# Attention and feed-forward on one core: attention pairs two at a time

## The chip, the cores and the metric

The kernel runs on one core of a Trainium2 chip. A core has five engines with queues of their own: TensorE (PE, matrix products into PSUM), VectorE (DVE), ScalarE (ACT), GpSimd (POOL) and SyncE (SP, which here only issues DMA transfers). Each works its own instructions off in the order in which the program gives them; semaphores make one wait for another. The metric is the device time of one execution in microseconds.

## The reference

Eight sequences of 448 tokens, with 12 heads of 64, all in 32-bit floats:

```
rmsnorm(x, g) = x / sqrt(mean(x*x) + 1e-6) * g
attn = softmax(rmsnorm(q, g_q) @ rmsnorm(k, g_k).T / sqrt(64)) @ v     # per sequence and head
x    = attn, the 12 heads side by side: 3584 tokens x 768
xn   = rmsnorm over the 768, times rms_g
g    = xn @ w_gate;  val = xn @ w_val                                # 768 x 1536 each
out  = (g * sigmoid(g) * val) @ w_out                                # 1536 x 768
```

## The kernel before

**Pairs.** Two heads of one sequence make a pair; g counts the 48 pairs, six to a sequence. Two heads fill the 128 rows of TensorE, so scores and values run as 64x64 products on quarters of its array, four at a time, while the feed-forward part uses the whole array.

**A step of the attention.** The 448 keys of a pair are cut in 7 parts. `step(g, i)` (L826) makes the scores of pair g for part i (L805), the weighted values of the pair before, g - 1, for the same part (L823), and, on ScalarE, the exponentials of the new scores (L813, or L811 from sequence 5 on, where q and k come in another layout, the "turned" one). So the values of pair g are added up while pair g + 1 is scored. One pair is seven such steps, 14 rows on TensorE, since a product of 32-bit floats takes two passes. Scores take PSUM banks from a pool of four (`ps_s`), the values the single bank of `ps_m`, which the transposes of q and k use too, and the feed-forward part three banks (`ps_f`). Exponentials take 11 buffers.

**Sums.** The denominators of the softmax are sums over all keys. GpSimd adds the seven exponentials of a pair into one tile (`later_sums`, L904 and L909: six additions), TensorE adds up the 128 rows (`totals`, L887, or in a folded form L867 after VectorE has folded the tile), and VectorE inverts them (L739 to L741). That is done at every even g for the two pairs before it. An odd pair's values are copied out of PSUM unscaled (`hold`, L772); an even step's are multiplied at once (`weigh`, L780), which also has ScalarE square the result and GpSimd add the squares up for the later norm (L783 to L786).

**Feed-forward.** While sequence b is in the attention, sequence b - 1 or the one before is in the feed-forward part, as a list of "products" (`todo`), each one to two microseconds of TensorE. `fill()` takes a sixteenth of a block's list, `fill(n)` takes n. From the second sequence on, gate and value products come from a scheme with 15 products in place of 18 for each of four groups (`three`, products L1419, evacuations L1434 to L1440, the last steps L1451 and L1452, called hand), and the output products from similar schemes with 7 in place of 8, once (`out_strassen`, L1693) or twice nested (`out_quads`, L1778). Both need sums of left operands, which VectorE makes ahead of them (L1492, L989 for x; L1610, L1638 for the output). Such sums are given to the queue one after a product, from the lists `first_sums` and `slow`. In the first sequences VectorE, ScalarE and GpSimd also convert the weights from 64-bit floats (`convert`, one step after each product).

**Time in steps.** `pe(fn)` counts one step, runs fn and then whatever `after(n, ...)` had put n steps ahead. `light(fn)` gives small work of VectorE to a list from which one is taken after each product; `hurry_light` empties it.

**The main loop** (L2143 to L2200) goes over g. For a pair inside a sequence: the attention of pair g, a `fill()`, the preparation of q and k of the next pairs, `fill()`, `fill()`. The last product before an even pair holds its conversion back until the first step of the attention. For the first pair of a sequence (hp = 0) comes the seam: the last ten products of the list (`LEFT = 10`) lie behind its attention, as 3, 2, 1 and the rest; between them stand the fold and the sum of the squares of x (`fold_x`, L922, and `rms_x`, L928 or L937), then `begin` puts the next block's list in place, `norm_x` (L949 or L953) spreads 1/rms, VectorE scales x (L959, six scalings), and a `fill()` follows.

**Places in SBUF.** One tile, `yard`, holds q, k, v and small rows at offsets written out by hand (`AT_...`). In the turned layout, the inverse norms of a pair (`rs`) stand in one of two places.

Of the kernel before, what the change touches and what calls it, by code (L numbers as in the profile page):

```python
# [8 lines left out]
F32 = mybir.dt.float32  # L9
# [326 lines left out]
def safe_scores(  # L336
# [85 lines left out]
    AT_QK = PER_B  # L422
    AT_V = AT_QK + 3 * PAIR
    AT_OTHER = AT_V + 3 * THIRD
    AT_RS = AT_V
    AT_V1 = AT_RS + 7 * NB
# [38 lines left out]
    def squares_turned(g):  # L465

        qk, n = st["qk", g], 2 * NB
        ms = st["ms", g] = spot(AT_RS, 2 * n).rearrange("p (a n) -> p a n", a=2)
        rs = st["rs", g] = spot(AT_RS + (4 + g % 2) * NB + g % 2 * NB // 2, NB + NB // 2)
# [345 lines left out]
    def weighted(g, i):  # L815

        b, hp = divmod(g, NPAIR)
        if i == 0:
            st["av", g] = ps_m.tile([128, 512], F32, name="av", tag="m")
        for j in range(2):  # L820
            r = across(j)
            vt = st["v", g][r, i] if turned(g) else st["vr", b][r, hp] if i == PARTS - 1 else st["v", g][r, i // NK, i % NK]
            nc.tensor.matmul(st["av", g][own(j), 0:S], lhsT=vt, rhs=st["e", g, i][r], start=i == 0, stop=i == PARTS - 1,  # L823
                             skip_group_check=True)

    def step(g, i):  # L826
# [2 lines left out]
        weighted(g - 1, i)  # L829
        if ps is not None:  # L830
            exps(g, i, ps)

    AT_ALIKE = AT_OTHER
    AT_FEW = AT_ALIKE + 128

    def late(g):

# [24 lines left out]
    def totals_folded(g):  # L862

        which = (g - 1, g)
        den = ps_s.tile([128, 512], F32, name="den", tag="s")[:, 0:2 * NB]
        for j in range(2):
            nc.tensor.matmul(den[own(j)], lhsT=alike()[across(j), own(j)], rhs=some_few(0, 2)[across(j)], start=True, stop=True)  # L867
        few = some_few(2, 2)
        nc.vector.reciprocal(few, den)
        for i in which:  # L870
            rd = st["rd", i] = tmp.tile([128, S], F32, name="rd", tag="rd", bufs=2)
            nc.vector.transpose(out=blocks(rd), in_=few[:, i % 2 * NB:(i % 2 + 1) * NB].unsqueeze(2).to_broadcast([128, NB, 32]))
            if i < g:
                weigh(i, 3, 4)

    def totals(g):

# [17 lines left out]
        for i in which[::-1]:  # L895
            invert(st["rd", i], st["rd", i])
            if i < g:
                weigh(i, 3, 4)

    def later_sums(g, n):  # L900

        def first():
            st["es", g] = tmp.tile([128, S], F32, name="es", tag="es", bufs=2)
            nc.gpsimd.tensor_tensor(st["es", g], st["e", g, 0], st["e", g, 1], ALU.add)  # L904
            more(2)

        def more(*parts):
            for i in parts:
                nc.gpsimd.tensor_tensor(st["es", g], st["es", g], st["e", g, i], ALU.add)  # L909

        after(n, first)
        after(n + 2, lambda: more(3, 4))
        after(n + 3, lambda: more(5, 6))
        if folded(g):
            after(n + 8, lambda: light(lambda: fold(g)))

# [1143 lines left out]
            convert()  # L2060


    at_once(squares(0, 0))
    warm(15)
    reduce, root, scale = norm_rests(0, 0, 2)
# [16 lines left out]
    for g in range(NG + 1):  # L2082
# [51 lines left out]
        if g == NPAIR + 1:  # L2134
# [8 lines left out]
            later_sums(g, 2)  # L2143
            begin(0, 15)
        else:
            hurry_light()
            sums_due = g % 2 == 0
            pe(lambda: (totals(g - 1) if sums_due else None, step(g, 0)))
            if st.pop("held", None):
                convert()  # L2150
            pe(lambda: [step(g, i) for i in (1, 2)])
            derive_q()
            pe(lambda: [step(g, i) for i in (3, 4)])
            pe(lambda: ([step(g, i) for i in (5, 6)], weigh(g - 1, 2) if sums_due else hold(g - 1)))
            if g < NG:
                later_sums(g, 11 if g == 3 * NPAIR else 2)
        st["block"] = now["t"]
        for n in (1, 2):
            if turned(g + n) == (n == 1):
                after(2, lambda g=g + n: load_v(g))  # L2160
        if hp:
            fill()
            norm_k(g + 1, 0)
            if not turned(g + 2):
                squares(g + 2, 0)
                squares(g + 2, 1)
            turn_for(g + 1, 0)
            if turned(g + 2):
                squares(g + 2, 0)
            norm_k(g + 1, 1)  # L2170
            some_rests(g)
            fill()
            turn_for(g + 1, 1)
            fill(hold=g % 2 == 1)
            continue
        fill(3)
        norm_k(g + 1, 0)
        if g == TURNED * NPAIR:
            one_per_quarter()
        fill(2)  # L2180
        if late(g):
            fold_x(b - 1)
        turn_for(g + 1, 0)
        norm_k(g + 1, 1)
        fill(1)
        if not late(g):
            pe(lambda: rms_x(b - 1))
        squares(g + 2, 0)
        squares(g + 2, 1)
        turn_for(g + 1, 1)  # L2190
        if late(g):
            fill(min(2, len(todo)))
            pe(lambda: rms_x(b - 1))
        fill(len(todo))
        begin(b - 1, 16)
        pe(lambda: norm_x(b - 1))
        fill()
    fill(len(todo))
    for _ in range(5):
        pe(idle)  # L2200
# [38 lines left out]
```

## Time and profile before

| | |
|---|---|
| Median of 3 runs | 1476.36 us (1475.61 to 1476.56) |
| Profiled execution | 1474.93 us, of which the span from the first to the last instruction is 1473.1 |
| Busy, TensorE | 1453.9 us (99%) |
| Busy, VectorE | 1073.0 us (73%) |
| Busy, GpSimd | 763.9 us (52%) |
| Busy, ScalarE | 620.1 us (42%) |
| DMA | 322.52 MB, 219 GB/s in the mean |
| Granted clock of TensorE | 0.999 |

The profile is one execution. A row of a timeline merges like instructions that follow each other on an engine: start in microseconds from the span's start, length, engine, line of the kernel, operation, output<-inputs by the program's names, shapes, and xcount. Where the engine was idle before it, a bracket gives for how long and what ended it. A row of the groups has the count, then the busy time in microseconds and the mean of one in nanoseconds, then the engine's idle time just before those instructions and what ended most of it. Matmuls are pipelined and their ends are modelled, so a row's length is more than its share of the stream: differences of starts are what counts on TensorE.

### The profile page before, as it was taken

How to read it: one execution, taken by the hardware profiler on the slowest of the kernel's cores; microseconds unless marked ns; L12 is line 12 of the kernel's file. 1: busy time of each engine (PE TensorE's matmuls, PEld its weight loads, DVE VectorE, ACT ScalarE, POOL GpSimd, SP SyncE). 2: the span in 40 equal slices, each digit the busy share in tenths (PEclk: the TensorE clock that was granted, in tenths of full speed). 3: DMA queues.
4: the chain of work that ended last, by engine and by line, in shares of the span. 5: the costliest groups of instructions: out<-in, count | busy, mean ns of one | idle time of the engine just before them, and what ended most of it. 6: DMA issues, size and time to landing. Idle time of an engine off the chain costs nothing.

```text
span 1473.1 us, 25744 instructions
## 1 busy us (share of the span) xinstructions
PE 1453.9 (99%) x8538; PEld 1142.2 (78%) x8538; DVE 1073.0 (73%) x1868; ACT 620.1 (42%) x1551; POOL 763.9 (52%) x684
## 2 busy tenths in 40 slices
PE   9999999999999999999999999999999999999998
PEld 4344445678855788887888889859898799899998
DVE  6788999799975677874579855755679755784665
ACT  7856776455423444234442443444542533101110
POOL 6867997647343363462545744655645842120003
PEclk9999999999999999999999999999999999999999
DMA  8758676776787999777656866677467855597576
GB/s 218 225 158 250 185 240 184 216 252 226 260 267 225 307 314 319 241 248 207 154 165 199 263 191 184 184 227 203 131 191 222 274 171 149 162 305 237 169 231 203
DMA packets 340577, 322.52 MB, mean 219 GB/s; under 512 B 126932, under 2 KB 282068, under 8 KB 340436
## 3 DMA queue, kind: packets, MB, share of 16 engines
q1 hardware_dynamic: 339428, 320.48, 72.9%
q8 instruction: 71, 1.16, 0.3%
q14 instruction: 70, 0.57, 0.1%
q10 hardware_dynamic: 880, 0.30, 0.1%
q0 software_dynamic: 128, 0.00, 0.0%
HBM read 266.90 MB, written 53.77 MB: 218 GB/s over the span
## 4 chain that ended last, share of the span: by engine, by line


## 5 line engine op out<-in xcount | busy, mean ns | idle before, releaser
L909 POOL TENSOR_TENSOR es<-es,e 128x448 f32<-128x448 f32 x205 | 254.5, 1241 | 13.6
L1419 PE MATMUL ff<-x,w 128*128 128x224 f32 x1296 | 258.1, 353 | 0.3 <-DVE pc L1440 0.3
L1419 PEld LDWEIGHTS ff<-x,w 128*128 128x128 f32 x1296 | 243.6, 190 | 3.5 <-issue 2.1
L805 PE MATMUL sc<-qT,kT 64*64 64x448 f32 x1176 | 231.5, 539 | 0.6 <-DVE x L959 0.5
L823 PE MATMUL av<-e,yard 64*64 64x448 f32 x1148 | 224.3, 538 | 0.0
L1419 PE MATMUL ff<-xs,w 128*128 128x224 f32 x832 | 164.5, 353 | 2.7 <-DMA w<-kept 1.9
L1419 PEld LDWEIGHTS ff<-xs,w 128*128 128x128 f32 x832 | 156.3, 190 | 6.2 <-issue 2.1
L805 PEld LDWEIGHTS sc<-qT,kT 64*64 64x64 f32 x1176 | 78.8, 133 | 87.2 <-issue 53.8
L786 POOL TENSOR_TENSOR ss<-ss,rd 128x448 f32<-128x448 f32 x40 | 47.7, 1192 | 157.8 <-ACT rd L785 156.4
L1778 PE MATMUL ff<-w,l 128*128 128x192 f32 x630 | 116.7, 328 | 2.8 <-DVE l L1638 2.2
L1440 DVE TENSOR_TENSOR pc<-ff,l 128x448 f32<-128x448 f32 x56 | 34.8, 622 | 108.7 <-PE ff L1419 85.8
L1869 PE MATMUL ff<-x,w 128*128 128x448 f32 x288 | 111.8, 541 | 0.0
L1778 PEld LDWEIGHTS ff<-w,l 128*128 128x128 f32 x630 | 103.8, 190 | 7.8 <-DVE l L1638 3.0
L823 PEld LDWEIGHTS av<-e,yard 64*64 64x64 f32 x1148 | 77.1, 133 | 36.9 <-issue 36.7
L904 POOL TENSOR_TENSOR es<-e 128x448 f32<-128x448 f32 x41 | 49.1, 1196 | 107.9 <-ACT e L813 79.4
L813 ACT ACTIVATE e<-sc 128x448 f32<-128x448 f32 x168 | 87.9, 548 | 36.7 <-PE sc L805 27.2
L1869 PEld LDWEIGHTS ff<-x,w 128*128 128x128 f32 x288 | 53.3, 190 | 51.1 <-issue 48.2
L811 ACT ACTIVATE e<-sc,yard 128x448 f32<-128x448 f32 x126 | 78.3, 635 | 31.8 <-PE sc L805 23.3
L1419 PE MATMUL ff<-top_x,w 128*128 128x224 f32 x440 | 91.1, 357 | 0.0
L1419 PEld LDWEIGHTS ff<-top_x,w 128*128 128x128 f32 x440 | 81.8, 190 | 11.5 <-issue 8.5
L1437 DVE TENSOR_TENSOR pb<-ff,pb 128x448 f32<-128x448 f32 x84 | 52.2, 622 | 48.9 <-PE ff L1419 48.8
L1736 POOL TENSOR_TENSOR y<-y,pa 128x384 f32<-128x384 f32 x10 | 11.1, 1128 | 144.8 <-DVE y L1844 137.2
(251 smaller groups left out, 2972.6 us busy)
## 6 DMA issues: line engine op xcount, KB each, us to landing
w<-kept SPq DMA_DIRECT2D x380, 256.0 KB, 3.9
w<-kept_q SPq DMA_DIRECT2D x350, 192.0 KB, 3.7
w<-kept_o SPq DMA_DIRECT2D x150, 192.0 KB, 4.0
kept_q<-w SPq DMA_DIRECT2D x63, 192.0 KB, 4.0
raw<-in_moe_w_gate_dram SPq DMA_DIRECT2D x24, 384.0 KB, 4.6
raw<-in_moe_w_val_dram SPq DMA_DIRECT2D x24, 384.0 KB, 4.2
kept<-w SPq DMA_DIRECT2D x48, 192.0 KB, 4.2
raw<-in_moe_w_out_dram SPq DMA_DIRECT2D x24, 384.0 KB, 3.7
```

Of the source, the lines that this page charges most:

```text
L786: after(m, lambda: (nc.gpsimd.tensor_tensor(ss, ss, rd, ALU.add), st.update({("summed", b): hp})))
L805: nc.tensor.matmul(ps[r, 0:S], lhsT=keys(g, r, i), rhs=st["qT", g][r, :], start=True, stop=True)
L811: nc.scalar.activation(e, ps[:, 0:S], ACT.Exp, scale=st["rs", g][:, NB + i:NB + i + 1])
L813: nc.scalar.activation(e, ps[:, 0:S], ACT.Exp)
L823: nc.tensor.matmul(st["av", g][own(j), 0:S], lhsT=vt, rhs=st["e", g, i][r], start=i == 0, stop=i == PARTS - 1, skip_group_check=True)
L904: nc.gpsimd.tensor_tensor(st["es", g], st["e", g, 0], st["e", g, 1], ALU.add)
L909: nc.gpsimd.tensor_tensor(st["es", g], st["es", g], st["e", g, i], ALU.add)
L1419: nc.tensor.matmul(bank[:, w * HT:(w + 1) * HT], lhsT=data(key)[:, (2 * w + c) * 128:(2 * w + c + 1) * 128], rhs=a[left][:, c, :], start=o ...
L1437: nc.vector.tensor_tensor(T[name], ps[:, 0:S], T[name], ALU.add)
L1440: nc.vector.tensor_tensor(T[name], ps[:, 0:S], T[other], what)
L1778: nc.tensor.matmul(ps, lhsT=a[:, j, :], rhs=data(key)[:, n % 2 * HW:(n % 2 + 1) * HW], start=start and j == 0, stop=j == KG - 1, skip_grou ...
L1869: nc.tensor.matmul(bank[w][:, 0:S], lhsT=data(key)[:, c * 128:(c + 1) * 128], rhs=st["x", 0][:, 3 * half + c, :], start=half == c == 0, st ...
```

## The change

Every even pair from 8 on now "leads" (`leads`): its attention waits until the products that stood behind it are done, and the attention of the next, odd pair follows at once, with no product between. So pairs 8 and 9, 10 and 11, up to 46 and 47 each share one excursion of 28 rows. Pair 7 and the last values (g = 48) stay alone.

- While a second pair is scored, the values of the first are added up in a bank of the scores' pool and not of `ps_m`, which still holds those of the pair before until they are scaled.
- A leading pair's additions on GpSimd are put in the queue during its own steps (`gap`, and `later_sums` ahead of `attend`); those of the second pair come two steps after, as before.
- The squares of scaled values are put off behind the excursion (7, or 8 and 9 steps in place of 2, or 3 and 4), except where a sequence's norm is about to need them.
- At the start of a sequence (pairs 12, 18, 24, 30, 36 and 42 lead there) five of the last ten products come ahead of the excursion; the other five, the fold, the sum and the scaling of x follow behind it, in the order in which they stood. The first pair's values are copied out of their bank only after the seam.
- The inverse norms of the turned layout get three places, since two pairs are in work at once; some offsets in `yard` move.

```diff
-            st["av", g] = ps_m.tile([128, 512], F32, name="av", tag="m")
+            st["av", g] = (ps_s if leads(g) else ps_m).tile([128, 512], F32, name="av", tag="s" if leads(g) else "m")
...
-                weigh(i, 3, 4)
+                weigh(i, *((8, 9) if leads(g + 1) and (g + 1) % NPAIR else (3, 4)))
...
+    def leads(g):
+
+        return g > NPAIR + 1 and g < NG and g % 2 == 0
...
+        gap = 1 if leads(g) else 2
         after(n, first)
-        after(n + 2, lambda: more(3, 4))
-        after(n + 3, lambda: more(5, 6))
+        after(n + gap, lambda: more(3, 4))
+        after(n + gap + 1, lambda: more(5, 6))
...
+    def attend(g):
+
+        hurry_light()
+        sums_due = g % 2 == 0
+        if leads(g):
+            later_sums(g, 2)
+        pe(lambda: (totals(g - 1) if sums_due else None, step(g, 0)))
+        if st.pop("held", None):
+            convert()
+        pe(lambda: [step(g, i) for i in (1, 2)])
+        derive_q()
+        pe(lambda: [step(g, i) for i in (3, 4)])
+        pe(lambda: ([step(g, i) for i in (5, 6)], weigh(g - 1, 7 if leads(g) and g % NPAIR else 2) if sums_due else
+                    hold(g - 1) if (g - 1) % NPAIR or not leads(g - 1) else None))
+        if g < NG and not leads(g):
+            later_sums(g, 11 if g == 3 * NPAIR + 1 else 2)
+
+    def seam(b, g):
+
+        if late(g):
+            fold_x(b - 1)
+            fill(2)
+        else:
+            fill(1)
+            pe(lambda: rms_x(b - 1))
+        squares(g + 2, 0)
+        squares(g + 2, 1)
+        if late(g):
+            pe(lambda: rms_x(b - 1))
+        fill(len(todo))
+        begin(b - 1, 16)
+        pe(lambda: norm_x(b - 1))
+        fill()
...
+        if leads(g) and not hp:
             hurry_light()
...
+            fill(3)
+            norm_k(g + 1, 0)
...
+            turn_for(g + 1, 0)
+            norm_k(g + 1, 1)
+            fill(2, hold=True)
+            turn_for(g + 1, 1)
+            attend(g)
+            attended(g)
+            continue
+        if hp == 1 and leads(g - 1):
+            seam(b, g - 1)
+            hold(g - 1)
         if hp:
+            hurry_light()
             fill()
...
-            fill(hold=g % 2 == 1)
+            fill(hold=leads(g) or g % 2 == 1 and not leads(g + 1))
+            if leads(g):
+                attend(g)
+                attended(g)
             continue
```

More of the change, by code (lines that the diff above doesn't have):

```diff
@@ L424, in safe_scores @@
     AT_OTHER = AT_V + 3 * THIRD
-    AT_RS = AT_V
-    AT_V1 = AT_RS + 7 * NB
+    AT_V1 = AT_V + 7 * NB
+    AT_ALIKE = AT_OTHER
+    AT_FEW = AT_ALIKE + 128
+    AT_RS = AT_FEW + 6 * NB
     yard = slots.tile([128, AT_OTHER + PER_B], F32, name="yard")
@@ L897, in totals @@
             if i < g:
-                weigh(i, 3, 4)
+                weigh(i, *((8, 9) if leads(g + 1) and (g + 1) % NPAIR else (3, 4)))
+    def leads(g):
+        return g > NPAIR + 1 and g < NG and g % 2 == 0
     def later_sums(g, n):
@@ L2060, in turns, with attended @@
             convert()
+    def attend(g):
[28 more added lines that the diff above has]
+        fill()
+    def attended(g):
+        for n in (1, 2):
+            if turned(g + n) == (n == 1):
+                after(2, lambda g=g + n: load_v(g))
+        st["block"] = now["t"]
     at_once(squares(0, 0))
@@ L2145, in safe_scores @@
         else:
-            hurry_light()
[L2147 to L2160, printed above, removed]
+            if not leads(g):
+                attend(g)
+        if not leads(g):
+            attended(g)
+        if leads(g) and not hp:
+            hurry_light()
+            fill(3)
+            norm_k(g + 1, 0)
+            if g == TURNED * NPAIR:
+                one_per_quarter()
+            turn_for(g + 1, 0)
[8 more added lines that the diff above has]
+            hold(g - 1)
         if hp:
+            hurry_light()
             fill()
@@ L2173, in safe_scores @@
             turn_for(g + 1, 1)
-            fill(hold=g % 2 == 1)
+            fill(hold=leads(g) or g % 2 == 1 and not leads(g + 1))
+            if leads(g):
+                attend(g)
+                attended(g)
             continue
[L2176 to L2197, printed above, removed]
+        fill(5)
+        seam(b, g)
     fill(len(todo))
```

4 lines of the change are left out of this document (1 added, 3 removed).

## The prediction

> **What bounds the kernel now.** I read the page first, then the timeline of TensorE around the attention, the idle stretches of VectorE, and the groups by line.
>
> ```profile
> span 1473.1 us, 25744 instructions
> PE 1453.9 (99%) x8538; PEld 1142.2 (78%) x8538; DVE 1073.0 (73%) x1868; ACT 620.1 (42%) x1551; POOL 763.9 (52%) x684
> ```
>
> TensorE is the bound: 99% of the span. A gain must shorten its own stream, and a delay on another engine costs only where TensorE runs out of something. The first thing to read is what a trip into the attention costs. Below, on TensorE, is pair 29's (columns: start, length, work, count; an idle time stands in brackets).
>
> ```profile
> 722.99 1.68 PE L1419 MATMUL ff<-top_x,w 128*128 128x224 f32 x8
> 724.60 0.59 PE L805 MATMUL sc<-qT,kT 64*64 64x448 f32 x2
> 725.02 0.54 PE L805 MATMUL sc<-qT,kT 64*64 64x448 f32 x2
> ...
> 729.53 0.54 PE L805 MATMUL sc<-qT,kT 64*64 64x448 f32 x2
> ...
> 730.02 1.78 PE L1419 MATMUL ff<-top_x,w 128*128 128x224 f32 x8
> 731.64 1.68 PE L1419 MATMUL ff<-x,w 128*128 128x224 f32 x8
> 733.15 3.19 PE L1419 MATMUL ff<-l,w 128*128 128x224 f32 x16
> ```
>
> No idle time is shown, and yet time goes. Eight instructions of a product take 1.51 us in the stream (731.64 to 733.15), so the attention was due at 724.50 and starts at 724.60: 0.10 lost. A row of the attention, two scores and two value instructions, takes 0.376 us (12 of them from 725.02 to 729.53); the first takes 0.42: 0.04 lost. The last row should end at 729.91 and the product starts at 730.02: 0.11. That product takes 1.62 and not 1.51: 0.11. One trip out and back costs **0.36 us** beyond its work.
>
> **The trips saved.** Pairs 8 to 47 now make 40 trips and will make 20: pair 8 with 9, up to 46 with 47. 20 x 0.36 = **7.2 us off**. No work of TensorE is added, nor any product removed. If the two halves of a merged trip did not join, the saving would be less; that is a rival below.
>
> **Inside a merged trip.** ScalarE must turn scores into exponentials faster than two rows (0.75 us) make them, now for 14 steps with one of four score banks given to the first pair's values in the second half.
>
> ```profile
> L813 ACT ACTIVATE e<-sc 128x448 f32<-128x448 f32 x168 | 87.9, 548 | 36.7 <-PE sc L805 27.2
> L811 ACT ACTIVATE e<-sc,yard 128x448 f32<-128x448 f32 x126 | 78.3, 635 | 31.8 <-PE sc L805 23.3
> 726.99 1.14 POOL L904 TENSOR_TENSOR es<-e 128x448 f32<-128x448 f32 x1 [6.28 <-ACT e L813]
> 728.20 6.26 POOL L909 TENSOR_TENSOR es<-es,e 128x448 f32<-128x448 f32 x5
> ```
>
> 0.55 or 0.64 against 0.75: ScalarE keeps up, and the squares that would have come between exponentials are put behind the trip (7, 8 and 9 steps), except at a sequence's end. A pair's six additions on GpSimd take 7.5 us (726.99 to 734.46). With 11 buffers for exponentials, the second pair's fifth exponential needs the first pair's first buffer, which GpSimd frees after its first addition, early in the trip. I cost the inside at nothing; if ScalarE or GpSimd enters late, it costs up to 0.4 us a trip (one exponential that finds no bank), 8 us in all.
>
> **The seams.** Six merged trips (pairs 12, 18, 24, 30, 36, 42 with the next) stand before a seam, where a sequence's attention output is normalised and the next block's products begin. Now a single trip stands before the last ten products and another some four output products behind them. The change puts five of the ten ahead, both trips together, and behind them the other five, the seam and all the output products with no trip among them. What did that second trip hide? Seam 30, TensorE and then VectorE:
>
> ```profile
> 773.60 1.78 PE L1419 MATMUL ff<-raw,w 128*128 128x224 f32 x8 [0.33 <-DVE pb L1437]
> 781.07 2.11 PE L1778 MATMUL ff<-w,h 128*128 128x192 f32 x12
> 788.53 2.22 PE L1778 MATMUL ff<-w,l 128*128 128x192 f32 x12
> 798.21 1.24 PE L1778 MATMUL ff<-w,l 128*128 128x192 f32 x6 [1.22 <-DVE l L1638]
> ...
> 769.62 0.63 DVE L922 STREAM_TRANSPOSE ss<-ss 128x448 f32<-128x448 f32 x1
> 776.88 0.58 DVE L1437 TENSOR_TENSOR pc<-ff,pc 128x448 f32<-128x448 f32 x1
> 797.59 0.56 DVE L1638 TENSOR_TENSOR l<-l,raw 128x384 f32<-128x384 f32 x1
> 800.46 0.36 DVE L1804 TENSOR_TENSOR th<-ff,th 128x192 f32<-128x192 f32 x1 [0.78 <-PE ff L1778]
> ```
>
> The wait at 798.21 is for VectorE's left operand of 797.59, and VectorE has no pause from the evacuation of product ten (776.88) until 800.46. It needs 21.2 us for that chain (to 798.1); the trip from 783.1 to 788.5 gives it 5.4 of them, and still TensorE loses 0.33 + 1.22 = 1.55 us here. Now the last seam, which has no trip behind it already:
>
> ```profile
> 1278.45 1.68 PE L1419 MATMUL ff<-raw,w 128*128 128x224 f32 x8
> 1294.72 2.11 PE L1778 MATMUL ff<-w,l 128*128 128x192 f32 x12
> ...
> 1280.17 0.62 DVE L1437 TENSOR_TENSOR pc<-ff,pc 128x448 f32<-128x448 f32 x1 [0.29 <-PE ff L1419]
> 1294.23 0.56 DVE L1638 TENSOR_TENSOR l<-l,raw 128x384 f32<-128x384 f32 x1
> ```
>
> There TensorE needs the operand 15.7 us after product ten (from 1279.97 to the second six of 1294.72, so 1295.7), and VectorE makes it in 14.5 (1280.17 to 1294.7). It just fits. The other seams carry five more scalings of x in that stretch, since only the last one spreads them out: 5 x 0.6 = 3.0 us. The 21.2 of today is the same 17.5 with about 4 us of collisions, which the groups show:
>
> ```profile
> L959 DVE SCALAR_TENSOR_TENSOR x<-x,rg,ss 128x448 f32<-128x448 f32 x24 | 24.8, 1068 | 0.0
> L959 DVE SCALAR_TENSOR_TENSOR x<-x,rg,rb 128x448 f32<-128x448 f32 x24 | 14.8, 671 | 1.8 <-PE rb L953 1.8
> ```
>
> The same scaling takes 671 ns with an input in PSUM and 1068 with all in SBUF, where it meets GpSimd's additions. In the changed kernel the second pair's additions (7.5 us) run behind the trip, about until product ten, so 0 to 4.0 us of collisions fall into the chain; I take 1.0, nearer the lower end since most of the additions meet evacuations, which read PSUM. The chain also starts late. GpSimd's two additions for the row sums of x stand behind the first pair's six, which begin where the rows of pair 26 show it:
>
> ```profile
> 632.92 0.98 PE L887 MATMUL den<-es,ones 64*64 64x448 f32 x8
> 636.58 1.14 POOL L904 TENSOR_TENSOR es<-e 128x448 f32<-128x448 f32 x1 [2.45 <-ACT e L813]
> ```
>
> That is 3.7 us into the trip, so the row sums are done at 3.7 + 7.5 + 2 x 1.2 = 13.6 us, and the merged trip takes 0.8 (denominators) + 28 x 0.376 = 11.3. The fold (769.62 and one more operation, 1.2 us together) starts 2.2 us behind the trip. With five evacuations and two reductions queued behind it, VectorE is 0 to 2.2 us late at product ten; I take 1.8, nearer the fold's own wait. TensorE itself waits 0.3 for the fold. At seam 30 the stall is 0.3 + 0.2 (from a product to its evacuation) + 1.8 + 17.5 + 1.0 - 15.7 = 5.1, less the 1.55 lost now: **+3.5**. Seam 42 loses 0.95 now: **+4.1**. Seam 24 has no fold on VectorE (1.2 less) and loses next to nothing now: **+3.9**. With collisions and lateness at their ends the stall is 2.0 to 8.5.
>
> The Trainium skill, "SBUF — State Buffer", section "Who interferes with whom", says that a VectorE instruction with two SBUF inputs and a GpSimd instruction that reads SBUF shut each other out for the whole instruction. By that rule six additions could hold up 7.5 us of the chain at each of three seams, and the sum would be 1480 + 3 x 6.5 = 1499; the rows agree in kind (671 against 1068), not in extent.
>
> Seam 36 is followed by larger output products:
>
> ```profile
> 955.39 2.10 PE L1693 MATMUL ff<-w,raw 128*128 128x384 f32 x6
> ...
> 956.55 0.56 DVE L1610 TENSOR_TENSOR raw<-raw,h 128x384 f32<-128x384 f32 x1
> ```
>
> The next six would start at 957.3 and read what VectorE has done by 957.1; with 0.2 to spare, 1.8 of lateness costs **+1.6**. Seams 12 and 18 have slack behind them and lose 0.51 and 1.12 now:
>
> ```profile
> 247.27 0.59 PE L805 MATMUL sc<-qT,kT 64*64 64x448 f32 x2 [0.51 <-DVE x L959]
> 402.62 1.78 PE L1419 MATMUL ff<-raw,w 128*128 128x224 f32 x8 [1.12 <-DVE pb L1437]
> 505.86 1.75 PE L1419 MATMUL ff<-xs,w 128*128 128x224 f32 x8 [0.97 <-DMA w<-kept]
> 1126.65 1.24 PE L1778 MATMUL ff<-w,l 128*128 128x192 f32 x6 [0.95 <-DVE l L1638]
> ```
>
> Those two go, against 0.4 of waiting for the row sums at each: **-0.8**. Of the small stalls elsewhere I let 1.4 us go, because the first pair's additions now meet a VectorE with little to do, and nothing (0) to 2 would be as good a guess: **-1.4**. Loads, stores and the turned order of the rows are only shifted; SP's queue gets nothing new to wait for.
>
> **Sum:** -7.2 + 3.5 + 4.1 + 3.9 + 1.6 - 0.8 - 1.4 = **+3.7** us. The profiled execution took 1474.93 (a span of 1473.1 and 1.8 around it) and would take 1478.6; the median of the runs, 1476.36, is 1.4 above it, which makes **1480.0**.
>
> **Rivals.**
> *The seams hold (not slower).* One mechanism: VectorE's chain from product ten to the third output block's operand. If lateness and collisions are near zero, seams 30, 42 and 24 cost 2.0 less 1.55, 0.95 and 0, together 3.5, and the rest is -2.2: 1476.4 - 7.2 + 1.3 = 1470.5. It decides from about 1.9 us of collisions, lateness and waiting together at each seam, where I took 0.3 + 1.8 + 1.0 = 3.1: there the net is zero. For it: the last seam runs without a pause of TensorE. Against: it has neither the scalings nor a pair's additions.
> *A wash, 1474 to 1478*: the same with 1.3 to 2.4 us.
> *Every addition collides*: a pair's six additions each hold VectorE's chain for their whole length, 6.5 more than my 1.0 at three seams, 1499. Against: about 4 of 7.5 us are lost now.
> *The trip starves.* ScalarE or GpSimd backlog at its start, or a join that waits: 20 x 0.4 = 8 us more, 1488. For it: one bank fewer, and VectorE and GpSimd near full in the conversion of the weights. Against: the exponentials' 0.2 us of idle time each.
> *Weights come late.* A stretch of products doubles; waits like that at 505.86 happen twice now. Two to four more of 0.97 make +2 to +4 on any case.
>
> **How the numbers follow.** Seams give back more than is saved: 0.43, own range 1477.5 to 1485. Seams hold: 0.29. A wash: 0.17. The trip starves, or weights late on top: 0.09. Every addition collides: 0.02. About 0.2% (3 us) is what a measurement of this kernel can tell from no change. Faster: seams hold, 0.29. Same: the wash and 0.10 of the forecast's lower end, 0.27. Slower: the rest, 0.44. The range takes in the rivals down to 1470 and up to 1487.
>
> **What would show it.** Right: 20 long trips of 28 rows without a gap, TensorE's idle time before lines 1419 and 1778 grown to some 5 us behind seams 24, 30 and 42, ended by VectorE, and VectorE without a pause there. Wrong: no such gaps; or gaps inside the trips before line 805; or trips that cost the same as before.

## The result and the profile after

| | before | after |
|---|---|---|
| Median | 1476.18 us (1474.88 to 1476.56, 5 runs) | 1510.89 us (1509.58 to 1512.44, 5 runs) |
| Ratio | | 1.0237, 95% interval 1.0223 to 1.0251 |
| Profiled execution | 1474.93 us, span 1473.1 | 1512.44 us, span 1510.5 |

Slower by 34.7 us, where 1480.0 was predicted with a range of 1470 to 1487. The page of the kernel after:

```profile
span 1510.5 us, 25813 instructions
PE 1459.3 (97%) x8538; PEld 1159.8 (77%) x8538; DVE 1053.3 (70%) x1868; ACT 617.9 (41%) x1551; POOL 757.5 (50%) x684
```

TensorE is busy 5.4 us more (1459.3 against 1453.9) and idle 32.0 us more (51.2 against 19.2 of the span). The trips themselves joined as forecast. On TensorE of the kernel after, pairs 28 and 29:

```profile
753.49 0.54 PE L825 MATMUL av<-e,yard 64*64 64x448 f32 x2
...
764.12 1.78 PE L1423 MATMUL ff<-top_x,w 128*128 128x224 f32 x8
```

28 rows run from 753.49 to 764.12, 0.38 each, with no idle time in them; the other 19 merged trips have no product inside them either. Where did the idle time come from? The busy time by stretch, in the kernel before (columns: from:to, length, busy time and count of each engine, granted clock of TensorE, share of the DMA engines, GB/s):

```profile
0.00:285.00 285.00, 280.78 (x1355) 136.10 (x1356) 234.49 (x387) 191.74 (x511) 228.99 (x223) 1.00 0.73 207
285.00:570.00 285.00, 280.23 (x1637) 218.56 (x1636) 225.21 (x393) 121.62 (x362) 133.42 (x122) 1.00 0.85 269
570.00:1473.10 903.10, 892.90 (x5550) 787.50 (x5548) 613.30 (x1090) 306.69 (x680) 401.50 (x339) 1.00 0.70 207
```

and in the kernel after, cut at about the same places of the program:

```profile
0.00:290.00 290.00, 284.09 (x1336) 145.93 (x1337) 236.97 (x395) 190.81 (x522) 223.11 (x220) 1.00 0.73 209
290.00:590.00 300.00, 274.74 (x1595) 207.24 (x1594) 218.88 (x373) 118.11 (x342) 130.17 (x121) 0.97 0.79 250
590.00:1510.50 920.50, 900.45 (x5611) 806.59 (x5609) 597.46 (x1102) 309.02 (x687) 404.25 (x344) 1.00 0.69 203
```

TensorE's idle time is length less busy: 4.2, 4.8 and 10.2 us before; 5.9, 25.3 and 20.0 after. So 20.5 of the 32 us arise between 290 and 590 us, and there alone the granted clock falls (0.97). Ahead of 290 us 1.7 are added, and 9.8 behind 590 us, where the four seams lie for which a loss was forecast. Five of the six waits of 2 us or more in the middle stretch, on TensorE of the kernel after:

```profile
314.71 3.26 PE L1423 MATMUL ff<-x,w 128*128 128x224 f32 x8 [3.03 <-DVE w L1318]
321.73 3.17 PE L1423 MATMUL ff<-raw,w 128*128 128x224 f32 x8 [3.77 <-DVE w L1318]
...
385.67 1.54 PE L1423 MATMUL ff<-raw 128*128 128x224 f32 x4 [2.24 <-DVE pb L1441]
...
440.74 1.65 PE L1697 MATMUL ff<-w,top 128*128 128x384 f32 x2 [3.49 <-DMA w<-kept_o]
...
476.80 1.59 PE L1697 MATMUL ff<-w,raw 128*128 128x384 f32 x4 [2.00 <-DMA w<-kept_o]
```

Two wait for a weight that VectorE has just made (L1318, in `derive`), one for an evacuation by VectorE (L1441), two for output weights to arrive. In this stretch the second and third blocks' weights are still prepared: gate weights of the second block are loaded, VectorE makes the sums of them that the scheme needs, the sums are stored for the later blocks, and the output weights go the same way. What VectorE did around the first two waits, in the kernel after:

```profile
308.69 0.62 DVE L1441 TENSOR_TENSOR pa<-ff,pa 128x448 f32<-128x448 f32 x1 [5.73 <-PE ff L1423]
...
313.06 1.50 DVE L1318 TENSOR_TENSOR w<-w,raw 128x512 f32<-128x512 f32 x1
318.00 1.16 DVE L1441 TENSOR_TENSOR pc<-ff,pc 128x448 f32<-128x448 f32 x2 [3.44 <-PE ff L1423]
...
320.98 0.69 DVE L1318 TENSOR_TENSOR w<-w,raw 128x512 f32<-128x512 f32 x1
```

VectorE stands still for 5.73 us in the merged trip and for 3.44 us behind it, and the two sums come just ahead of the products that need them (314.71 and 321.73). The second one stands in VectorE's queue behind the evacuation of the very product that waits for the first. `derive` is called from `fill` only, that is between trips, and there only from the third program step behind a trip on.

The wait at 440.74 has a like history, behind the merged trip of pairs 18 and 19 (406.1 to 416.7). VectorE stands still for 5.74 us in and behind that trip too, and makes the next sums of output weights (L1350) only from 427.76 on. SyncE's queue meanwhile holds at the store of such a sum (L1177), with the loads behind it. What that queue waited for between 400 and 480 us (in all, times, longest):

```profile
SPq L1177 <- DVE w L1350: 11.3, 5, 8.9
```

The 8.9 us end at 429.27, and the next loads of output weights are issued from 435.27 on. The DMA engines are busy for only 0.45 of the time between 420 and 440 us, so these loads are late by their issue. In the kernel before, the longest wait of that queue for such a sum was 3.6 us between 290 and 570.

### The profile page after: what moved, and what is told of

It is laid out like the page before. It is cut to its first block, busy times and chain, and to the rows that moved or that the text cites. A ratio compares the mean times of both kernels' runs of the same rounds, so it can differ in the third digit from the quotient of the medians.

```text
span 1510.5 us, 25813 instructions
## 1 busy us (share of the span) xinstructions
PE 1459.3 (97%) x8538; PEld 1159.8 (77%) x8538; DVE 1053.3 (70%) x1868; ACT 617.9 (41%) x1551; POOL 757.5 (50%) x684
## 4 chain that ended last, share of the span: by engine, by line
## 5 line engine op out<-in xcount | busy, mean ns | idle before, releaser
L1423 PE MATMUL ff<-x,w 128*128 128x224 f32 x1296 | 261.2, 355 | 9.3 <-DVE w L1318 3.0
L912 POOL TENSOR_TENSOR es<-es,e 128x448 f32<-128x448 f32 x205 | 247.3, 1206 | 14.4
L825 PE MATMUL av<-e,yard 64*64 64x448 f32 x1148 | 220.3, 537 | 0.9 <-ACT kT L697 0.9
L815 ACT ACTIVATE e<-sc 128x448 f32<-128x448 f32 x168 | 87.9, 546 | 23.1 <-PE sc L807 19.2
L1441 DVE TENSOR_TENSOR pb<-ff,pb 128x448 f32<-128x448 f32 x84 | 52.2, 622 | 59.7 <-PE ff L1423 59.0
L1423 PE MATMUL ff<-top_x,w 128*128 128x224 f32 x432 | 88.0, 355 | 0.0
L1801 ACT COPY th<-ff 128x192 f32<-128x192 f32 x35 | 11.1, 318 | 179.2 <-PE ff L1782 154.8
L1423 PE MATMUL ff<-l,w 128*128 128x224 f32 x416 | 83.6, 353 | 0.0
```

The source lines that it names most:

```text
L815: nc.scalar.activation(e, ps[:, 0:S], ACT.Exp)
L1423: nc.tensor.matmul(bank[:, w * HT:(w + 1) * HT], lhsT=data(key)[:, (2 * w + c) * 128:(2 * w + c + 1) * 128], rhs=a[left][:, c, :], start=o ...
L1441: nc.vector.tensor_tensor(T[name], ps[:, 0:S], T[name], ALU.add)
L1801: nc.scalar.copy(q1, ps[:, 0])
```

## The experiments

Three theories stood against each other. *Preparation*: the loss is the chain that makes and loads weights between 290 and 570 us. *Seams*: VectorE's chain behind all six seams, as predicted. *Starving*: a merged trip costs in itself. In these kernels a pair that doesn't lead takes the path of the kernel before; the diffs show only the rest. (In e12, where none leads, the trips start within 0.2 us of where they start in the kernel before up to 480 us, and again from 600 to 783.) Each median stands beside that of the kernel before, run along with it.

| run | merged | median, us | before | ratio, 95% interval |
|---|---|---|---|---|
| e1 | all from 20 on | 1491.87 | 1475.61 | 1.0107, 1.0090 to 1.0124 |
| e2 | inside sequences | 1492.65 | 1475.61 | 1.0112, 1.0095 to 1.0129 |
| e3 | inside, from 20 on | 1482.51 | 1475.61 | 1.0044, 1.0027 to 1.0060 |
| e4 | all, sums in the trip | 1496.78 | 1475.61 | 1.0150, 1.0133 to 1.0167 |
| e5 | inside, from 26 on | 1469.89 | 1475.12 | 0.9969, 0.9958 to 0.9980 |
| e6 | all from 24 on | 1480.28 | 1475.12 | 1.0031, 1.0019 to 1.0043 |
| e7 | e6, x spread | 1473.15 | 1475.12 | 0.9990, 0.9981 to 1.0000 |
| e8 | e3, half gate loads | 1476.73 | 1475.12 | 1.0012, 1.0002 to 1.0021 |
| e9 | 14 alone | 1488.40 | 1474.87 | 1.0106, 1.0085 to 1.0127 |
| e10 | e9, idle filled | 1489.57 | 1474.87 | 1.0096, 1.0080 to 1.0111 |
| e11 | e5, x spread at 30, 36, 42 | 1471.55 | 1474.87 | 0.9979, 0.9970 to 0.9988 |
| e12 | none, x spread at 30, 36, 42 | 1481.17 | 1474.87 | 1.0043, 1.0028 to 1.0058 |
| e13 | e9, sums in the trip | 1476.46 | 1475.39 | 1.0007, 0.9998 to 1.0017 |
| e14 | e9, idle filled, half as much | 1486.22 | 1475.39 | 1.0077, 1.0062 to 1.0093 |
| e15 | e3, half gate and output loads | 1473.61 | 1475.39 | 0.9989, 0.9980 to 0.9998 |
| e16 | e5, x spread at 30 and 42 | 1468.49 | 1475.39 | 0.9955, 0.9942 to 0.9969 |

### Where: some trips only (e1 to e3)

```
     def leads(g):
-        return g > NPAIR + 1 and g < NG and g % 2 == 0
+        return g > NPAIR + 1 and g < NG and g % 2 == 0 and g >= 20                # e1
+        return g > NPAIR + 1 and g < NG and g % 2 == 0 and g % NPAIR              # e2
+        return g > NPAIR + 1 and g < NG and g % 2 == 0 and g % NPAIR and g >= 20  # e3
```

> Only pairs 20 to 47 are merged (14 trips, seams 24, 30, 36 and 42 among them); pairs 8 to 19 run as in the kernel before. Preparation theory (the loss lies between 290 and 570 us, where the second block's gate weights and the output weights are still made, stored and loaded, and the single trips gave that chain time): 14 x 0.36 = 5.0 us saved, and only the seams' stalls stay, 3.9 at seam 24, 3.85 - 1.55 = 2.3 at seam 30, 0.9 at seam 36 and 3.25 - 0.95 = 2.3 at seam 42, together +9.4; so 1476.2 + 4.4 = 1480.6, up to 1485 if the loads at 530 to 565 us still come late. Seam theory (VectorE's chain at all six seams holds the whole 34.7 + 7.2 = 41.9 us, 7 a seam): four seams give 28, 1499. Starving theory (41.9 over 20 trips, 2.1 each): 14 x (2.1 - 0.36) = +24, 1500.

> Only the 14 trips inside a sequence are merged (8, 10, 14, 16, 20, 22 and so on); the six seams are as in the kernel before, their two trips apart. Saved 14 x 0.36 = 5.0. Preparation theory: the two stalls of 3.0 and 3.8 us at 314 and 321 us stand behind the merged pairs 14 and 15, so they stay in part, with the half clock behind them: about half of the 28 us of that stretch, 1476.2 - 5.0 + 14 = 1485 (1478 to 1495). Seam theory: no seam is merged, 1476.2 - 5.0 = 1471.2. Starving theory: 14 x 1.7 = +24, 1500.

> Only the ten trips inside a sequence from pair 20 on are merged (20, 22, 26, 28, 32, 34, 38, 40, 44, 46); seams and pairs 8 to 19 as in the kernel before. Saved 10 x 0.36 = 3.6. Preparation theory and seam theory both: 1472.6; if the loads at 530 to 565 us belong to merging pairs 20 to 23 and not to what was late before them, up to 4 more, 1476.6. Starving theory: 10 x 1.7 = +17, 1493.

e2 merges no seam and is still 17 us slower, so the seam theory can't hold the loss; the two waits of 3.0 and 3.8 us are there unchanged. e3, with ten trips that touch neither a seam nor the second block's sums, should have been 1472.6 by two theories and came out 10 higher; e1 likewise, 11 higher than expected. So my preparation theory was too narrow. TensorE of e3, the four largest of five waits for gate weights, 7.5 us in all:

```profile
513.41 3.27 PE L1423 MATMUL ff<-xs,w 128*128 128x224 f32 x16 [2.25 <-DMA w<-kept]
...
526.32 1.75 PE L1423 MATMUL ff<-x,w 128*128 128x224 f32 x8 [1.64 <-DMA w<-kept]
529.76 5.10 PE L1423 MATMUL ff<-x,w 128*128 128x224 f32 x24 [1.69 <-DMA w<-kept]
...
544.37 1.75 PE L1423 MATMUL ff<-xs,w 128*128 128x224 f32 x8 [1.61 <-DMA w<-kept]
```

These are loads of gate weights that come late. The stretches of the kernel *before* suggest a reason, in the last but one column:

```profile
500.00:540.00 40.00, 37.70 (x228) 31.85 (x227) 31.45 (x64) 16.62 (x37) 15.40 (x16) 1.00 0.98 309
...
560.00:580.00 20.00, 20.00 (x139) 15.81 (x138) 14.03 (x32) 11.30 (x24) 1.77 (x3) 1.00 1.01 322
...
600.00:700.00 100.00, 99.22 (x680) 82.35 (x679) 67.92 (x124) 38.10 (x89) 48.65 (x47) 1.00 0.76 228
```

The DMA engines are full in the first two, 0.98 and 1.01, and yet TensorE is idle for only 2.3 of 40 us in one and not at all in the other. A trip reads no weights. Two trips drawn together leave a longer stretch of products in a row, and the loads, with few buffers to run ahead into, could fall behind. That is the loads theory of the next runs.

### The loads (e5, e8, e15)

```
-            nc.sync.dma_start(out=data(key)[:, 0:src.shape[-1]], in_=src)
+            w = src.shape[-1] // (2 if key[0:2] == ("wg", 2) else 1)                # e8
+            w = src.shape[-1] // (2 if key[0:2] in (("wg", 2), ("wo", 1)) else 1)   # e15
+            nc.sync.dma_start(out=data(key)[:, 0:w], in_=src[:, 0:w])
```

e5 is e3's edit with 26 in place of 20. e8 loads only the first half of each gate weight of the third sequence, and e15 also only half of each output weight of the second; the rest of the buffer keeps what stood there, and the products are as many as before.

> Eight trips inside a sequence are merged, from pair 26 on (26, 28, 32, 34, 38, 40, 44, 46); seams and pairs 8 to 25 as in the kernel before. Loads theory (formed on the run with ten trips from pair 20 on, which lost 10 us at 450 to 575 us, where the DMA engines are 0.95 to 1.03 busy in the kernel before too: a trip reads no weights, and two trips drawn together leave a longer stretch of products than the loads can keep up with): from 600 us on the DMA share is 0.76 and less, no load is late, 8 x 0.36 = 2.9 saved, 1475.6 - 2.9 = 1472.7. Starving theory (merging itself costs, about 1 us a trip as in that run): 1475.6 + 8 x 0.7 = 1481.

> The run with ten trips merged inside sequences from pair 20 on, with only half of each gate weight of the third sequence loaded (the other half holds what stood there before); all else, the products too, is as it was. That takes 128 KB from each of these loads, the ones that came late at 509 to 545 us (7.5 us in all). Loads theory (the DMA engines' throughput in that stretch): those waits go, and what stands behind them (2.9 us at VectorE's sums behind) in part: 1482.5 - 7 to - 9, about 1474.5. If the loads are late because they are issued late (a buffer that comes free late, SP's queue held by another store): unchanged, 1482.5.

> Ten trips inside a sequence merged from pair 20 on, with only half of each gate weight of the third sequence and half of each output weight of the second loaded (the rest holds what stood there). Loads theory: besides the gate waits, the waits for output weights at 454 to 466 us (3.3 us) go too: 1476.7 - 3 = 1473.5. If these wait for VectorE's sums and stores of the output weights instead: unchanged, 1476.7.

All three came out in the direction of the loads theory. e5 is faster than the kernel before by 5.2 us, more than the 2.9 expected: in the profiled executions TensorE is busy 4.2 us less (0.52 a trip and not 0.36) and idle 1.5 less (17.7 against 19.2), about half of that at places that the edit leaves alone; I didn't resolve that further. Between e3 and e5 lie only the merges of 20 with 21 and 22 with 23, and 12 us. With half the gate loads the gate waits shrink from 7.5 us to 1.9, on TensorE of e8:

```profile
523.42 4.78 PE L1424 MATMUL ff<-x,w 128*128 128x224 f32 x24 [0.51 <-DMA w<-kept]
528.72 1.75 PE L1424 MATMUL ff<-x,w 128*128 128x224 f32 x8 [0.51 <-DMA w<-kept]
...
539.29 1.75 PE L1424 MATMUL ff<-xs,w 128*128 128x224 f32 x8 [0.93 <-DMA w<-kept]
```

and the median falls by 5.8 (7 to 9 were expected, since waits for output weights at 454 to 466 us stayed). Halving those as well (e15) took 3.1 more, with 3 expected. So it is the bytes to be moved in that stretch that the trips of e3 ran into. Loads whose size was left alone land sooner too: in e8 those of output weights take 3.9 us from issue to landing, in e3 5.0 (medians, 505 to 545 us). That some loads were also issued late is not ruled out, since a halved load that is issued late lands sooner as well.

### Sums in the trip (e4, e9, e13)

e9 merges pair 14 with 15 alone (`g == 14`). e4 and e13 add calls in a merged trip; e4 to the whole change, one after steps 1 and 2, e13 to the single merge, one more after steps 3 and 4:

```
         derive_q()
+        if leads(g) or leads(g - 1):
+            derive()                       # e4: and derive_o()
         pe(lambda: [step(g, i) for i in (3, 4)])
+        if leads(g) or leads(g - 1):       # e13 only
+            derive()
```

> The changed kernel, with VectorE's sums for the gate weights and for the output weights (one of each) also started in the middle of each half of a merged trip, where only those of the quartered output weights were started. Nothing is left out. Preparation theory, in the form that these sums are held back by the order of the program, not by a lack of time on VectorE: the stalls at 314, 321, 440 and 476 us (12.3 us idle, and 4 stretches of half clock of 1.7 each, 6.8) shrink by most of their 19 us, to 1492 to 1497. If VectorE, the buffers or the loads were short and not the order: unchanged, 1511. Seam theory and starving theory: unchanged, 1511, or a little slower since VectorE has more to do in the trip.

> One trip alone is merged, pair 14 with 15; all else as in the kernel before. Preparation theory: the two stalls behind that trip (3.0 and 3.8 us idle, and two stretches of 3.4 us at half clock, 1.7 each) come with this one merge: 1475.3 - 0.4 + 10.2 = 1485; up to 4 more if the stall of 2.2 at 385 us and its half clock come too, and up to 3 less since later loads then have more time: 1482 to 1489. If the stalls come from the sum of what the merges before it put off: 1475 to 1478.

> Pair 14 merged with 15 alone, as before, and VectorE's sums for the gate weights also started in the middle and towards the end of each half of that trip; the two sums that TensorE waited for (3.0 and 3.8 us) are then issued seven to nine program steps ahead of their products instead of one. Order theory: both stalls and the half clock behind them go; of the 13.5 us most come back: 1476 to 1479. If VectorE's time, a buffer or the loads were short: 1486 to 1488.

One merge costs 13.5 us by itself, at the upper end of what was expected, and nearly all of it comes back when the same sums are put in the queue some steps earlier: 1476.46. Nothing else differs between e9 and e13, so it is the order of the program, not a lack of VectorE's time, of a buffer or of a load. VectorE of e13, two of the sums:

```profile
297.59 1.33 DVE L1315 TENSOR_TENSOR w<-w,raw 128x512 f32<-128x512 f32 x1
...
302.05 1.51 DVE L1318 TENSOR_TENSOR raw<-raw 128x512 f32<-128x512 f32 x1
```

The sums now run between 297.59 and 305.1, where VectorE stood still for 5.74 us in e9, and TensorE's next products show no wait:

```profile
306.95 1.68 PE L1423 MATMUL ff<-x,w 128*128 128x224 f32 x8
308.46 1.68 PE L1423 MATMUL ff<-raw 128*128 128x224 f32 x8
```

In the whole change (e4) a like edit brings back 14 us (1510.9 to 1496.8); waits for loads stay, the longest 3.04 and 2.25 us.

### The seams (e6, e7, e11, e12, e16)

e6 merges all from 24 on; e7 also spreads the scalings of x:

```
-            if b == B - 1:
+            if b > 3:                      # e7, e11, e12
+            if b in (4, 6, B - 1):         # e16
                 slow.append(("x", lambda hp=hp: scale(hp)))
...
-        while left not in a:
+        while left not in a or slow and slow[0][0] == "x":
             slow.pop(0)[1]()
```

> Twelve trips merged, all from pair 24 on, seams 24, 30, 36 and 42 among them; pairs 8 to 23 as in the kernel before. Loads theory together with the seams' stalls as the changed kernel showed them: 12 x 0.36 = 4.3 saved, the seams cost 3.9, 2.3, 0.9 and 2.3, together 9.4: 1475.6 + 5.1 = 1480.7. If merging costs by itself wherever it is done (1 us a trip): 1475.6 + 12 x 0.7 + 9.4 = 1493.

> The same twelve trips, and at seams 30, 36 and 42 the six scalings of x stand one by one behind later products, as the last seam alone had them; seam 24 keeps them together. Chain theory (VectorE's chain from product ten to the third output block's operand sets the seams' stalls, and five scalings of 0.6 us or more stand in it): 3.0 us or more come back at seams 30 and 42 and the 0.9 at seam 36, so 1480.7 - 6.9 = 1473.8; seam 24 still loses 3.9. If the stall is set by something else (loads, GpSimd's sums): no change, 1480.7.

> The eight trips from pair 26 on that lie inside a sequence are merged, and the scalings of x at seams 30, 36 and 42 stand one by one behind later products. Chain theory: the waits of seam 30 (0.33 and 1.22) and of seam 42 (0.95) go: 1469.9 - 2.5 = 1467.4. If at single trips the scalings get in the way of the next products' evacuations: 1469.9 or a little more.

> No trip is merged; only the scalings of x at seams 30, 36 and 42 are spread as in the run with eight merged trips. 1475.3 - 2.5 = 1472.8, and the difference to that run is what the eight merges are worth without seams: 2.9 at 0.36 each, 5.2 as they measured.

> Eight trips from pair 26 on inside a sequence merged, the scalings of x spread at seams 30 and 42 and not at 36. If the parts add up: 1469.9 - 2.5 = 1467.4, with no wait of TensorE left behind seams 30 and 42 but the 0.33, and none at 979 to 995 us (2.8 with seam 36 spread). Otherwise 1470 as without the spreading.

e6 and e7 came within 0.7 us of the chain theory, e6 in part by luck (see below). Seam 30 on TensorE, e6 first:

```profile
778.52 0.36 PE L932 MATMUL msx<-yard 128*128 128x14 f32 x2 [0.64 <-DVE yard L927]
...
792.96 2.22 PE L1782 MATMUL ff<-w,l 128*128 128x192 f32 x12 [1.64 <-DVE pa L1831]
...
796.50 1.24 PE L1782 MATMUL ff<-w,h 128*128 128x192 f32 x6 [0.35 <-DVE y L1802]
...
803.41 1.24 PE L1782 MATMUL ff<-w,l 128*128 128x192 f32 x6 [1.22 <-DVE l L1642]
```

then e7, with the scalings out of the way:

```profile
791.90 2.22 PE L1782 MATMUL ff<-w,l 128*128 128x192 f32 x12 [0.44 <-DVE pa L1831]
...
800.15 1.24 PE L1782 MATMUL ff<-w,l 128*128 128x192 f32 x6 [0.19 <-DVE l L1642]
```

Of 3.21 us behind the fold's 0.64, 0.63 are left. Spreading without merging (e12) was a miss: 6 us slower than the kernel before where 2.5 faster was expected. At seam 36, which has fewer output products to put scalings behind, the next block's products now wait; e11 shows the same place:

```profile
979.42 6.32 PE L1423 MATMUL ff<-xs,w 128*128 128x224 f32 x32 [1.46 <-DVE xs L993]
991.32 3.27 PE L1423 MATMUL ff<-l,w 128*128 128x224 f32 x16 [1.04 <-ACT yard L488]
994.90 2.35 PE L1423 MATMUL ff<-x,w 128*128 128x224 f32 x11 [0.32 <-DVE x L993]
```

That is 2.8 us, and it answers for most of e11, which was 4 above what was expected. e12 shows waits at the other two seams too that e11 doesn't show: 0.49 and 0.89 us behind seam 30, 0.50 and 0.90 behind seam 42, more than the 1.22 and 0.95 that went. With 2.5 at seam 36 that is about half of what it lost; the rest isn't settled. e16 leaves seam 36 alone: **1468.49**, ratio 0.9955 (0.9942 to 0.9969), the fastest of all kernels here and 6.9 us below the kernel before; 1467.4 was expected.

### The half clock (e10, e14)

```
+        if b == 1 and g == GROUPS[0] and right in ("v10", "v13"):
+            bridge(a[left], 13 if right == "v10" else 16)     # e10; e14: 6 and 8
         for w in range(2):
...
+    def bridge(rhs, n):
+        ps = ps_s.tile([128, 512], F32, name="warm", tag="s")
+        for _ in range(n):
+            nc.tensor.matmul(ps[:, 0:HT], lhsT=ident, rhs=rhs[:, 0, :], start=True, stop=True)
```

> The same one merge, with 13 and 16 products of no use (128x128 by 128x224, 0.19 us each, into a score bank that nobody reads) ahead of the two products that wait there, so that TensorE works through 2.5 of 3.0 and 3.0 of 3.8 us of its two stalls. The sums that it waits for come no earlier. If the half clock comes from TensorE's idle time: both stretches stay at full clock, 3.4 us less than with the merge alone. If it comes from something else: the same time as with the merge alone, within 0.5 us.

> Pair 14 merged with 15 alone, with 6 and 8 calls of useless products ahead of the two that wait (each call 0.38 us as it was measured, so 2.3 of 3.0 and 3.0 of 3.8 us). Nothing that is waited for comes earlier. If idle time of TensorE brings the half clock on, and the half clock costs what the two products and the transpositions then take longer (1.2, 1.6 and 0.6): full clock throughout and 3.0 to 3.4 us less than 1488.4, 1485. If the half clock is not paid for in the end: 1488.4.

The two waiting products of e9, on TensorE:

```profile
310.11 2.75 PE L1423 MATMUL ff<-x,w 128*128 128x224 f32 x8 [3.02 <-DVE w L1318]
...
316.63 3.36 PE L1423 MATMUL ff<-raw,w 128*128 128x224 f32 x8 [3.77 <-DVE w L1318]
```

From 310.72 to 320.96 us the granted clock is a half. The windows of that stretch (the granted clock is the last column but two):

```profile
307.31:310.72 3.41, 0.61 (x3) 0.64 (x4) 2.62 (x3) 2.72 (x16) 3.25 (x3) 1.00 0.16 59
310.72:314.13 3.41, 2.14 (x7) 1.39 (x5) 1.23 (x3) 0.00 (x0) 1.72 (x5) 0.50 0.50 154
314.13:317.55 3.42, 0.92 (x3) 0.85 (x4) 2.37 (x4) 0.00 (x0) 0.00 (x0) 0.50 0.03 13
317.55:320.96 3.41, 3.41 (x12) 3.08 (x11) 0.94 (x2) 0.09 (x1) 0.00 (x0) 0.50 0.17 64
```

In e10 the clock is 1.00 throughout the program, but the time didn't fall: each call makes two instructions of 0.19 us (x26 for 13 calls), so 13 calls took 4.9 us and not 2.5, and the waiting products came later than without, at 311.79 and 319.36. e14 with half as many, on TensorE:

```profile
307.16 2.43 PE L1416 MATMUL warm<-x,ident 128*128 128x224 f32 x12
310.36 1.75 PE L1431 MATMUL ff<-x,w 128*128 128x224 f32 x8 [0.77 <-DVE w L1318]
311.95 3.19 PE L1416 MATMUL warm<-raw,ident 128*128 128x224 f32 x16
315.88 1.78 PE L1431 MATMUL ff<-raw,w 128*128 128x224 f32 x8 [0.74 <-DVE w L1318]
```

The products take 1.75 and 1.78, where e9's took 2.75 and 3.36, the clock stays full, and the median is 2.2 us lower than e9's (3.0 to 3.4 were expected; the intervals of the two overlap, so the size is not settled, only that idle time brings the half clock on).

## Why the prediction was wrong

- **The trips saved, 20 x 0.36.** Right. In e6, where the clock stays full until TensorE is done, TensorE is busy 4.1 us less for twelve merges (1449.8 against 1453.9), 0.34 each. In e5 eight trips were worth more.
- **Inside a merged trip nothing.** Right but for the first three: in the kernel after they have 1.8 us of idle time inside, ended by ScalarE, and the other seventeen 0.25 together. *The trip starves* (1488) is out: the time after lies above it, but e13 takes one merge's whole cost away without touching the trip's own work.
- **Seams 24, 30, 42 and 36.** The mechanism was right: VectorE ends nearly all of the waits, and the five scalings are most of it, 2.6 of the 3.0 us that the prediction gave them come back at seam 30. The size was over: 13.1 us were forecast for the four, and in e6 their waits of 0.3 us and more grow by 7.5 (3.85 at seam 30 where 5.1 was forecast, 2.5 at seam 24 where it was 3.9). The terms mis-sized are the collisions and the lateness, which one the runs don't say. Seam 24 did not lose next to nothing before, but 0.51 us at 651.04. And e6's 1480.7 rests on 9.4 for the seams, with 1.35 us counted to seam 24 that lie ahead of its trip and that e6 doesn't show; with 7.5 it would be 1478.8, so part of the agreement is luck.
- **"Seams 12 and 18 have slack behind them", -0.8, and "Loads, stores and the turned order of the rows are only shifted; SP's queue gets nothing new to wait for."** These are the steps that failed. The waits of 0.51 and 1.12 did go, but SyncE's queue got 8.9 us in one piece to wait for, behind seam 18, and TensorE 3.49 and 2.00 us for output weights. Differences of the runs to the kernel before give the price: six merged seams cost 34.7 - 17.0 = 17.7 us (the whole change less e2), the four later ones 16.3 - 6.9 = 9.4 (e1 less e3), so seams 12 and 18 some 8. The merges inside sequences up to pair 17 cost 17.0 - 6.9 = 10 (e2 less e3), those of pairs 20 to 23 some 12 (e3 less e5), and the other eight give 5 back. In idle time the stretch between 290 and 590 us lost 20.5 us, and some 8 to the half clock.
- **What is shown of the causes.** Merging pairs 14 and 15 alone costs 13.5, by the order in which the sums of the weights are started (shown by e9 and e13; that it is more than the 10 of all four early merges says that the parts don't simply add). Pairs 20 to 23 lose by loads that come late in a stretch of full DMA engines (shown by e3, e8 and e15). For seam 18 the chain from the late sum over SyncE's queue to TensorE is read from the trace, and no run tests it alone; for seam 12 the cause stays open.
- **Weights come late, "+2 to +4".** The rival named the right thing with the wrong size. It was priced by the two waits of 0.97 that stood in the profile, as if there were room up to them. The DMA share of that stretch, 0.98 and 1.01 in the kernel before, says that there was none; I had the slices of the page and read them for TensorE.
- ***Every addition collides*, 1499.** Nearest of the rivals in time and wrong in place. By the rule of the Trainium skill that it rests on ("SBUF — State Buffer", "Who interferes with whom"), each of three seams would have lost 6.5 us more than my 5.1; seam 30 lost 3.85.
- ***The seams hold*, 1470.5.** Its sum leaves out that seam 24 has no fold (1.2 less); by its own terms it comes to 1469.3.
- **What isn't explained.** The busy time of TensorE grew by 5.4: 7.2 less for trips and about 8 more for the half clock leave some 4.6, part of which is the slower start behind a wait (1.75 for a product in place of 1.68). The wait of 2.24 at 385.67 is in e2 too, where seam 18 is not merged, so it isn't that seam's: from 376.97 VectorE works without a pause up to the evacuation at 385.00 that TensorE waits for, and five operations for sums of gate weights (L1315, L1318) stand in between.

## What to carry to other kernels

A stretch of work on the bounding engine that needs no loads and little of a second engine is cover for both, and a profile without idle time doesn't show whom it covers: before moving it, list what the program starts between its pieces, and read the DMA share stretch by stretch, since 1.01 without a wait can be a bound about to show. Where work for a second engine is started only between such pieces, drawing them together can starve what comes next; with that work started inside them, one merge came out 1.1 us above the kernel before and not 13.5 (e13). And such a change may pay in one part of a kernel and cost in another: eight of the twenty merges, with the scalings at two seams spread, gave 0.45%, all twenty cost 2.4%.

## What was unexpected of the hardware

**A wait of 2 us can cost half the clock.** The half clock comes in pieces of 3.41 us whose starts lie whole multiples of 3.41 us apart (314.35, 321.18, 386.03, 440.65 and 478.19 in the kernel after: 2, 19, 16 and 11 of them). Cut along that grid, the kernel after shows:

```profile
310.94:314.35 3.41, 0.74 (x4) 0.39 (x3) 2.60 (x3) 2.48 (x12) 3.17 (x4) 1.00 0.51 174
314.35:317.77 3.42, 3.06 (x8) 2.53 (x8) 0.21 (x1) 0.75 (x7) 2.68 (x5) 0.50 0.53 153
...
529.39:532.81 3.42, 2.31 (x11) 1.65 (x10) 3.32 (x9) 1.35 (x3) 0.00 (x0) 1.00 1.08 371
532.81:536.22 3.41, 1.66 (x9) 1.69 (x10) 1.20 (x5) 0.19 (x1) 0.00 (x0) 1.00 1.03 372
536.22:539.63 3.41, 3.41 (x20) 3.41 (x19) 0.00 (x0) 1.27 (x3) 0.00 (x0) 1.00 0.97 307
```

2.67 us idle in one piece, and the next runs at half clock. A wait of 2.13 us that ends at 534.56 lies across two pieces, with 1.11 and 1.75 us of idle time, and neither is followed by one at half clock. In e2 a wait of the same 2.13 us falls into one piece (534.67 to 538.09), and the next one is at half clock. The least idle time that was followed by one, in e8:

```profile
463.13:466.54 3.41, 1.48 (x5) 0.62 (x4) 0.00 (x0) 0.00 (x0) 0.00 (x0) 1.00 1.00 325
466.54:469.96 3.42, 3.42 (x7) 1.75 (x6) 1.62 (x3) 0.00 (x0) 0.00 (x0) 0.50 0.80 260
```

So for a piece at full clock the limit lies near 1.9 us of idle time, somewhat more than half of it: all pieces up to 1.79 us (e14, 348.40 to 351.81) were followed by full clock. It is not sharp in these rows, since a piece with 1.99 us at the very end of e10 (1480.07) was not followed by half clock. A piece that is itself at half clock can be followed by another with less: the second of the rows of e9 above has 1.27 us. A wait's price thus depends on where it falls: up to 1.7 us more for the piece behind it, half of its length. The Trainium skill, "TensorE: Matmul & The Clock Gate", section "Part 1: The HAM clock gate (the "warmup" mystery)", has a free-running window of that length, and the half clock after one idle window. The traces agree with the length (3.41 us), but here little more than half a window of idle time was enough.
